# Holding back the later activation loads until the second third of a weight has landed

## The chip, the core and the metric

The kernel runs on one core of a Trainium2 chip. The metric is the device time of the whole kernel in microseconds (us). The engines are called PE (TensorE matmul), PEld (its weight loads), DVE (VectorE), ACT (ScalarE), POOL (GpSimd) and SP (SyncE, which here only issues transfers). PE's granted clock is the share of its full clock that it was given (1.00 is full). Before the change the median was 204.94 us over three runs, 204.71 to 204.94.

## The reference, cut to what matters

```python
xn = layernorm(x)                                  # x: 2048 tokens x 640
return x + linear_attention(xn, wqkv, wo) + gelu(xn @ w1 + b1) @ w2 + b2
```

The first 60 us of the kernel, the stage that the change touches, compute `gelu(xn @ w1 + b1)`, with `w1` of 640 x 1536. All numbers are bf16.

## The kernel before

The 2048 tokens are 16 tiles of 128. Tile t is loaded ("x*t*"), DVE computes its statistics and normalises it, the result is transposed (tiles 0 to 2 on PE, tiles 3 to 15 by a transposing DMA that SP issues), and PE multiplies it with W1. W1 comes in three thirds; the first is split over two queues. SP issues nearly all of it on its own queue, in this order:

```python
def dma_x(t, n):                       # x tiles t .. t+n-1, one DMA
    src = xv[t * P:(t + n) * P, :].rearrange("(t p) d -> p t d", p=P)
    Pl.ins("sync", lambda e: e.dma_start(x_in[:, t:t + n, :], src), writes=r_x[t:t + n], dma=True)
...
dma_x(0, 1)
dma_w("scalar", b1tmp[:], ...)                                   # ACT's queue
dma_w("scalar", W1[:, 0:KA, 0:FW], ..., r_W1A)                   # ACT's queue
dma_x(1, 1)
dma_w("sync", W1[:, KA:DT, 0:FW], ..., r_W1[0])                  # rest of the first third
dma_w1(1)                                                        # second third, 640 KB
dma_x(2, 1)
dma_w1(2)                                                        # last third, 640 KB
dma_x(3, 1)
dma_x(4, 2)                                                      # 320 KB
dma_x(6, 2)                                                      # 320 KB
dma_x(8, 4)                                                      # 640 KB
```

The rest of this stage in program order (DVE ran its part in this order in the trace of the kernel before: the statistics of tile 3 at 11.14 us, the first half of tile 4's at 12.64, the normalisation of tile 3 at 13.10):

```python
units(0, 2, JQ, 2 * JQ + 1)      # PE: tiles 0,1 with the second third (and one block of the last)
ln_stats(2)                      # DVE
ln_norm(2)
ln_stats(3)
xnT_copy(2, transp(2))           # PE transposes tile 2, DVE copies it
units(0, 2, 2 * JQ + 1, JT)
ln_next(3)                       # DVE: half statistics of tile 4, normalise tile 3, other half
xnT_dma(3)                       # SP: transposing DMA of tile 3
units(2, 1, 0, 10)               # PE: tile 2
units(3, 1, 0, 10)               # PE: tile 3, needs that DMA
units(2, 2, 10, JT)
for t in range(4, NT):           # DVE and SP: statistics, normalise, transposing DMA
    ...
units(4, 2, 0, 9)
...
```

Of the kernel before, what the change touches and what calls it, by code (L numbers as in the profile page):

```python
# [112 lines left out]
def bass_parallel_sum__linear_attn_block__dense_activation_gelu__prompt_kernel(  # L113
# [16 lines left out]
    Pl = Planner(nc)  # L130
# [7 lines left out]
    with contextlib.ExitStack() as es:  # L138
# [81 lines left out]
        r_W1 = [R_("W1_%d" % i) for i in range(NW1)]  # L220
# [30 lines left out]
        def dma_x(t, n):  # L251
            src = xv[t * P:(t + n) * P, :].rearrange("(t p) d -> p t d", p=P)
            Pl.ins("sync", lambda e: e.dma_start(x_in[:, t:t + n, :], src),
                   writes=r_x[t:t + n], dma=True)
# [7 lines left out]
        def dma_w1(i, eng="sync"):  # L262
            dma_w(eng, W1[:, :, i * FW:(i + 1) * FW], w1v[:, :, i * FW:(i + 1) * FW], r_W1[i])
# [7 lines left out]
        dma_x(2, 1)  # L271
        dma_w1(2)
        dma_x(3, 1)
        dma_x(4, 2)
        dma_x(6, 2)
        dma_x(8, 4)
# [555 lines left out]
```

## Time and profile before

| what | before |
|---|---|
| median time, three runs | 204.94 us |
| profiled span | 203.0 us |
| PE busy | 199.1 us, 98% |
| start of the first W1 product | 6.32 us |

The first fence is from the page of the kernel before: busy time of each engine, and the shares of the chain that ended last.

```profile
PE 199.1 (98%) x1317; PEld 121.8 (60%) x1329; DVE 123.0 (61%) x238; ACT 72.8 (36%) x139; POOL 14.4 (7%) x43
...
PE 96%; DVE 1%; DMA 1%; issue 0%; DVEq 0%
```

The second is the same chain in order of time (start us, length us, what).

```profile
0.80 2.27 DMA xPK<-in_A_x_dram
...
6.32 0.94 PE ps L407 x14
...
12.20 18.14 PE ps L375 x215
...
196.55 4.67 PE ps L726 x51
...
201.25 0.29 DVE out_l L729
```

The kernel waits for x0, normalises it, and from 6.32 us on the chain is PE's own work. So the time can change only if that run starts at another moment or gets a hole.

Next, the stretches of one microsecond (columns: stretch and its length; busy time of PE, PEld, DVE, ACT, POOL with instruction counts; granted PE clock; DMA share; GB/s), while the loads come in:

```profile
9.00:10.00 1.00, 1.00 (x13) 0.91 (x11) 0.90 (x3) 1.00 (x5) 0.22 (x1) 1.00 1.10 359
10.00:11.00 1.00, 1.00 (x12) 0.89 (x11) 0.24 (x2) 0.85 (x3) 0.57 (x1) 1.00 1.06 360
13.00:14.00 1.00, 1.00 (x14) 0.92 (x13) 0.94 (x3) 0.85 (x3) 0.40 (x1) 1.00 0.60 199
14.00:15.00 1.00, 1.00 (x22) 1.00 (x19) 0.95 (x3) 1.00 (x5) 0.66 (x2) 1.00 0.14 32
```

The transfers run at 360 GB/s until x8-11 drains at about 13.5 us. Last, SP's issue of x8-11 in the timeline (start, length), its time from issue to landing in the DMA view, and DVE's timeline around tile 4 (L331 statistics, L352 normalisation; the lines at 11.14, 12.64 and 13.10 are statistics of tile 3, first half of tile 4, and normalisation of tile 3):

```profile
5.93 0.98 SPq L253 DMA_DIRECT2D xPK<-in_A_x_dram  x1
```
```profile
xPK<-in_A_x_dram SPq DMA_DIRECT2D x1, 640.0 KB, 8.7
```
```profile
11.14 0.89 DVE L331 BATCH_NORM_STATS2 stats<-xPK 128x6 f32<-128x320 bf16 x2
12.64 0.48 DVE L331 BATCH_NORM_STATS2 stats<-xPK 128x6 f32<-128x320 bf16 x1
13.10 0.45 DVE L352 TENSOR_SCALAR xn_tm<-xPK,aggr,rstd 128x640 bf16<-128x640 bf16 x1
```

A line without brackets at its end had no wait worth noting before it: tile 4 was there when DVE came to it.

### The profile page before, as it was taken

The numbers are of one execution on the slowest core, as the hardware profiler recorded it, in microseconds if no ns is written. First come the engines' busy times: TensorE is split into PE (matmuls) and PEld (weight loads), VectorE is DVE, ScalarE is ACT, GpSimd is POOL, SyncE is SP. The second block draws the span as 40 slices with busy tenths as digits, with TensorE's granted clock in tenths as the row PEclk, the third lists the DMA queues.
The fourth block names the chain that finished last, engine by engine and source line by source line (L and its number), as shares of the span: only waits on it lengthen the run. The fifth ranks groups of instructions, "written<-read, shape, count | busy, mean of one in ns | idle before, by whom it ended". The sixth has DMA issues, their size and how long they took to land.

```text
span 203.0 us, 3442 instructions
## 1 busy us (share of the span) xinstructions
PE 199.1 (98%) x1317; PEld 121.8 (60%) x1329; DVE 123.0 (61%) x238; ACT 72.8 (36%) x139; POOL 14.4 (7%) x43
## 2 busy tenths in 40 slices
PE   7999999999999999999999999999999999999996
PEld 2799884444457777777756565444444444447775
DVE  4789682000006888999468899896793385356322
ACT  3589886666666544211143596100000000000000
POOL 3145443000000000000000000000000000000000
DMA  5975985999800000000289435115551966084402
GB/s 174 360 259 114 149 181 110 351 275 294 188 0 3 0 0 3 0 0 3 43 273 322 77 66 108 39 29 125 110 116 39 207 106 129 27 196 93 161 32 65
DMA packets 48134, 24.51 MB, mean 121 GB/s; under 512 B 33702, under 2 KB 48118, under 8 KB 48118
## 3 DMA queue, kind: packets, MB, share of 16 engines
q1 hardware_dynamic: 46094, 23.44, 46.4%
q10 hardware_dynamic: 2024, 0.86, 1.7%
q8 instruction: 10, 0.16, 0.3%
q14 instruction: 6, 0.05, 0.1%
HBM read 12.72 MB, written 2.62 MB: 76 GB/s over the span
## 4 chain that ended last, share of the span: by engine, by line
PE 96%; DVE 1%; DMA 1%; issue 0%; DVEq 0%
PE ps L748 27%; PE ps L375 25%; PE ps L524 11%; PE ps L557 11%; PE ps L569 11%; PE ps L690 7%; PE ps L726 2%; PE ps L407 1%; DMA xPK<-in_A_x_dram 1%; DVE stats L331 1%; PE ps L583 1%; PE ps L601 1%; PE ps L396 0%; DVE xn_tm L389 0%; DVE out_l L729 0%
## 5 line engine op out<-in xcount | busy, mean ns | idle before, releaser
L375 PE MATMUL ps<-xnT,W 128*128 128x256 bf16 (+2 forms) x372 | 50.2, 296 | 0.2
L375 PEld LDWEIGHTS ps<-xnT,W 128*128 128x128 bf16 x375 | 32.4, 98 | 17.3
L379 ACT ACTIVATE HG<-ps,b1c 128x256 bf16<-128x256 f32 (+2 forms) x75 | 37.3, 522 | 13.1 <-PE ps L375 11.3
L748 PE MATMUL ps<-HG,W 128*128 128x512 bf16 x177 | 39.2, 379 | 0.2
L748 PEld LDWEIGHTS ps<-HG,W 128*128 128x128 bf16 x180 | 17.6, 98 | 21.2
L569 PE MATMUL ps<-xnT,Wqkv 128*128 128x512 bf16 x96 | 22.2, 379 | 0.2
L524 PE MATMUL ps<-Wqkv,xnT 128*128 128x320 bf16 x160 | 21.9, 299 | 0.0
L557 PE MATMUL ps<-xPK,xn_tm 128*128 128x320 bf16 x160 | 21.9, 299 | 0.0
L524 PEld LDWEIGHTS ps<-Wqkv,xnT 128*128 128x128 bf16 x160 | 15.7, 98 | 6.2
L557 PEld LDWEIGHTS ps<-xPK,xn_tm 128*128 128x128 bf16 x160 | 15.7, 98 | 6.1
L754 DVE SCALAR_TENSOR_TENSOR W<-ps,b2c,xnT 128x512 bf16<-128x512 f32 x15 | 11.3, 751 | 8.9 <-PE ps L748 8.8
L748 PE MATMUL ps<-PQ,Msb 128*128 128x512 bf16 x73 | 16.4, 379 | 0.1
L569 PEld LDWEIGHTS ps<-xnT,Wqkv 128*128 128x128 bf16 x100 | 11.3, 118 | 8.5
L331 DVE BATCH_NORM_STATS2 stats<-xPK 128x6 f32<-128x320 bf16 x32 | 13.7, 468 | 4.4 <-DMA xPK<-in_A_x_dram 4.4
L508 ACT ACTIVATE xn_tm<-ps 128x512 bf16<-128x512 f32 x20 | 11.9, 597 | 9.4 <-PE ps L569 8.7
L511 DVE SCALAR_TENSOR_TENSOR PQ<-ps,xn_tm 128x512 bf16<-128x512 f32 x20 | 13.8, 692 | 2.1
L508 ACT ACTIVATE ek<-ps 128x640 bf16<-128x640 f32 x16 | 11.2, 703 | 9.2 <-PE ps L524 9.2
L511 DVE SCALAR_TENSOR_TENSOR xPK<-ps,ek 128x640 bf16<-128x640 f32 x16 | 13.2, 825 | 1.7
L516 DVE CAST b2c<-out_l 128x5 f32<-128x5 bf16 x1 | 0.2, 172 | 22.4 <-DMA out_l<-b2bc 22.4
L748 PEld LDWEIGHTS ps<-PQ,Msb 128*128 128x128 bf16 x75 | 7.3, 98 | 8.8
L618 DVE SCALAR_TENSOR_TENSOR xn_tm<-PQ,z_sb,xn_tm 128x512 f32<-128x512 bf16 x16 | 12.0, 750 | 0.4
L544 DVE TENSOR_TENSOR Msb<-Msb,xPK 128x640 f32<-128x640 f32 x14 | 11.6, 826 | 0.5
(64 smaller groups left out, 136.1 us busy)
## 6 DMA issues: line engine op xcount, KB each, us to landing
xPK<-in_A_x_dram SPq DMA_DIRECT2D x5, 640.0 KB, 6.9
Wqkv<-in_A_wqkv_dram SPq DMA_DIRECT2D x3, 800.0 KB, 7.0
W<-in_B_w_dram SPq DMA_DIRECT2D x1, 1920.0 KB, 14.8
out_dram<-xPK SPq DMA_DIRECT2D x3, 640.0 KB, 3.6
W<-in_B_w_dram SPq DMA_DIRECT2D x2, 640.0 KB, 6.7
xPK<-in_A_x_dram SPq DMA_DIRECT2D x4, 320.0 KB, 5.9
Wo<-in_A_wo_dram SPq DMA_DIRECT2D x1, 750.0 KB, 11.6
xPK<-in_A_x_dram SPq DMA_DIRECT2D x4, 160.0 KB, 4.4
```

What stands on the lines that cost most here:

```text
L331: Pl.ins(v, lambda e: e.bn_stats(stats[:, s, 6 * h:6 * h + 6], x_in[:, t, h * HW:(h + 1) * HW]), reads=[r_x[t]], writes=[r_stats[s][h]])
L375: Pl.ins("tensor", [(lambda e, k=k: e.matmul(bank(b, 0, w), W1[:, k, jb * P:(jb + 1) * P], xnT[:, k, tok], start=(k == 0), stop=(k == DT - ...
L379: Pl.ins("scalar", lambda e: e.activation(HG[:, jb, tok], bank(b, 0, w), ACT.Gelu_apprx_tanh, bias=b1c[:, jb:jb + 1]), reads=[B_[b], r_b1c ...
L508: Pl.ins("scalar", lambda e: e.activation(e2, src, ACT.Exp), reads=br, writes=[re])
L511: Pl.ins(v, lambda e: e.scalar_tensor_tensor(out=d2, in0=src, scalar=0.0, in1=e2, op0=ALU.max, op1=ALU.add), reads=br + [re], writes=[res_ ...
L524: fns.append(lambda e, k=k, h=h, b=b, t=t: e.matmul(bank(b + h, 0, HW), xnT[:, k, t * P:(t + 1) * P], Wqkv[:, k, D + h * HW:D + (h + 1) * ...
L544: Pl.ins(v, lambda e, t=t: e.tensor_tensor(out=zsum, in0=zsum, in1=PK[:, t, :], op=ALU.add), reads=[r_PK[t], r_zsum], writes=[r_zsum])
L557: Pl.ins("tensor", [(lambda e, t=t, h=h, b=b, f=f: e.matmul(bank(b + h, 0, HW), xn_tm[:, t, f * P:(f + 1) * P], PK[:, t, h * HW:(h + 1) * ...
L569: Pl.ins("tensor", [(lambda e, k=k, j=j, b=b: e.matmul(bank(b), Wqkv[:, k, j:D:DT], xnT[:, k, cc], start=(k == 0), stop=(k == DT - 1))) fo ...
L618: Pl.ins(v, lambda e: e.scalar_tensor_tensor(out=yv[c % 2], in0=pq, scalar=z_sb[:, j:j + 1], in1=yv[c % 2], op0=ALU.mult, op1=ALU.add), re ...
L690: return lambda e: e.matmul(bank(b + h, 0, HW), l, r[:, h * HW:(h + 1) * HW], start=(i == 0), stop=(i == JT + DT - 1))
L748: Pl.ins("tensor", lambda e, l=l, r=r, i=i: e.matmul(bank(b), l, r, start=(i == 0), stop=(i == JT + DT - 1)), reads=rd, writes=[B_[b]], ma ...
```

## The change

The idea is to keep 1280 KB of activations, which are needed later, from competing with W1 and x3, which are needed first. The diff is one line:

```diff
         dma_x(2, 1)
         dma_w1(2)
         dma_x(3, 1)
+        Pl.wait_event("sync", r_W1[1].w)
         dma_x(4, 2)
         dma_x(6, 2)
         dma_x(8, 4)
```

SP now stops after issuing x3 until W1's second third has landed, that is, until that load's semaphore has been raised 16 times. No byte and no instruction of another engine is added.

## The prediction

> **What bounds the kernel now.** TensorE. The page gives PE 199.1 of 203.0 us (98%). The chain of waits is 96% PE: from 6.32 us to the last eviction at 201.22 it is one unbroken run of matmuls, with only "issue" gaps of 0.05 us. The waits view lists a single PE wait, 1.3 us for the warm-up memset. Before that the chain is the load of x tile 0 (lands 3.07), statistics, normalisation, transposes. Only the start of that run, or a bubble in it, can move the time.
>
> **What the change does.** It adds one semaphore wait on SyncE, before the issue of x4-5, x6-7, x8-11 (1280 KB). The order view shows SP's instructions unchanged but for that wait. No byte is added or removed.
>
> Before, from the SP timeline and the DMA landing times (issue start + time to landing):
> - W1's second third: 2.2 + 6.1 = 8.3
> - x2: 2.73 + 6.1 = 8.8
> - W1's last third: 3.30 + 7.4 = 10.7
> - x3: 3.85 + 7.3 = 11.1
> - x4-5: 4.78 + 7.2 = 12.0; x6-7: 5.40 + 7.5 = 12.9; x8-11: about 6.0 + 8.7 = 14.7
>
> They land in the order of issue, spaced by their size at 360 GB/s (the windows view, flat from 6 to 13 us). [...] So x4 to x11 stand *behind* everything that the change wants to favour; they take no bandwidth from it. I expect no earlier landing of W1 or x3 (under 0.2 us), and PE waits for none anyway. (W1's last third is first needed near 11.2 us.)
>
> **After.** SP stalls from about 4.75 to 8.4, then issues the three loads with the same durations (0.58, 0.6, about 0.9): done near 10.6. An unloaded load takes 2.3 us to land in this trace (x0), of which about 1.2 us pass before data moves. So x4's packets are queued by about 9.6 us, while x3 and W1's last third still move. No hole opens in the DMA stream, or one of a few tenths. Landings: x4-5 12.0 to 12.3, x6-7 12.9 to 13.2, x8-11 14.6 to 15.0.
>
> **Slack.** DVE starts statistics of tile 4 at 12.64, of tile 6 at about 15.5, of tile 8 at 18.1: slack 0.6, 2.6, 3.5 us. SP's next work, the transposing load of tile 3, is issued at 13.57, after SP is free again (10.6). It lands at 16.3 and is needed by PE near 17.1. Nothing reaches PE.
>
> **Predicted:** 204.9 us, range 204.4 to 205.5. Faster by over 2%: 0.5%; within 2%: 99%; slower: 0.5%.
>
> **Right or wrong in the profile after:** start of the first W1 matmul still 6.3 us; W1 thirds and x3 land within 0.2 us of before; SP's three load issues begin near 8.4; DMA rate still about 360 GB/s to 13 us, with no slot below 250; statistics of tile 4 start within 0.3 us of 12.64; PE's waits view stays a single entry; everything from 20 us on is shifted by under 0.3 us.
>
> **What would make it wrong.** If a re-issued load takes far longer to get its first packet moving than 2.3 us, x4 lands after 13.3, DVE falls behind, the transposes of tiles 4 and 5 slip past PE's need near 20 us, and up to 1 us is lost. If queued loads do disturb those ahead of them, the first stage ends some tenths earlier.

That argument is the order of the landings in the trace (8.3, 8.8, 10.7, 11.1, 12.0, 12.9, 14.7 us) and their spacing at 360 GB/s; that the loads behind take no bandwidth was the inference from it. The forecast's 1.2 us before data moves is an estimate too; for x0 the trace has 1.04 us (0.80 to 1.84).

## The result, and the profile after

The changed kernel took 204.82 us (median of six runs, 204.64 to 205.88) against 204.92 us (six runs, 204.71 to 205.18). Ratios here are the mean time of one kernel's fast runs over the mean of the other's fast runs of the same rounds, so not quite the ratio of those medians: it is 1.0005, with a 95% interval of 0.9983 to 1.0027. Two more sets of timed rounds, on other occasions, gave 0.9996 (0.9974 to 1.0018) and 1.0011 (0.9989 to 1.0034). The change makes no difference that these runs can resolve.

The page's lines after the change, which answer to the first fence:

```profile
PE 200.2 (98%) x1329; PEld 121.9 (60%) x1329; DVE 123.0 (60%) x238; ACT 72.9 (36%) x139; POOL 14.4 (7%) x43
...
PE 96%; DVE 1%; DMA 1%; issue 0%; DVEq 0%
```

PE's larger busy sum is the 12 matmul records that are missing before (1317 of 1329), not more work. SP's waits show the new wait (us in total, times, longest):

```profile
SPq L253 <- DMA W<-in_B_w_dram: 3.7, 1, 3.7
```

SP's issue of x8-11 in the timeline, and its landing in the DMA view:

```profile
9.77 0.47 SPq L253 DMA_DIRECT2D xPK<-in_A_x_dram  x1
```
```profile
xPK<-in_A_x_dram SPq DMA_DIRECT2D x1, 640.0 KB, 5.6
```

So it is issued 3.8 us later (5.93 to 9.77), and lands 0.7 us later (5.93 + 8.7 = 14.6; 9.77 + 5.6 = 15.4). The queue's backlog has swallowed most of the delay. The same stretches as before:

```profile
9.00:10.00 1.00, 1.00 (x15) 0.92 (x13) 0.68 (x2) 1.00 (x5) 0.10 (x1) 1.00 0.91 289
10.00:11.00 1.00, 1.00 (x12) 0.90 (x10) 0.41 (x2) 0.91 (x3) 0.52 (x2) 1.00 0.92 272
13.00:14.00 1.00, 1.00 (x13) 0.91 (x11) 0.99 (x4) 0.92 (x2) 0.81 (x2) 1.00 0.94 324
14.00:15.00 1.00, 1.00 (x22) 1.00 (x20) 0.90 (x4) 0.94 (x4) 0.24 (x2) 1.00 0.23 86
```

The transfer rate dips between 9 and 11 us (289 and 272 GB/s against 359 and 360), and the missing bytes come after 13 us. DVE around tile 4:

```profile
11.64 0.88 DVE L332 BATCH_NORM_STATS2 stats<-xPK 128x6 f32<-128x320 bf16 x2
13.10 0.48 DVE L332 BATCH_NORM_STATS2 stats<-xPK 128x6 f32<-128x320 bf16 x1
13.59 0.45 DVE L353 TENSOR_SCALAR xn_tm<-xPK,aggr,rstd 128x640 bf16<-128x640 bf16 x1
```

Here everything is 0.5 us later than before, and still without a wait for tile 4. Something ahead of tile 4 was late. That something is x2: DVE waits for it in front of tile 2's statistics, in the kernel before and in the one after:

```profile
8.81 0.89 DVE L331 BATCH_NORM_STATS2 stats<-xPK 128x6 f32<-128x320 bf16 x2 [0.52 <-DMA xPK<-in_A_x_dram]
```
```profile
9.32 0.89 DVE L332 BATCH_NORM_STATS2 stats<-xPK 128x6 f32<-128x320 bf16 x2 [0.84 <-DMA xPK<-in_A_x_dram]
```

Whether the change did it was the first question for the experiments.

### The profile page after: what moved, and what is told of

Same layout as the page of the kernel before. It is cut to its first block, busy times and chain, and to the rows that moved or that the text cites. A ratio compares the mean times of both kernels' runs of the same rounds, so it can differ in the third digit from the quotient of the medians.

```text
span 203.4 us, 3454 instructions
## 1 busy us (share of the span) xinstructions
PE 200.2 (98%) x1329; PEld 121.9 (60%) x1329; DVE 123.0 (60%) x238; ACT 72.9 (36%) x139; POOL 14.4 (7%) x43
## 4 chain that ended last, share of the span: by engine, by line
PE 96%; DVE 1%; DMA 1%; issue 0%; DVEq 0%
PE ps L749 27%; PE ps L376 25%; PE ps L558 11%; PE ps L525 11%; PE ps L570 11%; PE ps L691 7%; PE ps L727 2%; PE ps L408 1%; DMA xPK<-in_A_x_dram 1%; DVE stats L332 1%; PE ps L584 1%; PE ps L602 1%; PE ps L397 0%; DVE xn_tm L390 0%; PE ps L319 0%
## 5 line engine op out<-in xcount | busy, mean ns | idle before, releaser
L570 PE MATMUL ps<-xnT,Wqkv 128*128 128x512 bf16 x100 | 22.8, 379 | 0.0
L749 PE MATMUL ps<-PQ,Msb 128*128 128x512 bf16 x75 | 16.7, 379 | 0.0
L512 DVE SCALAR_TENSOR_TENSOR xPK<-ps,ek 128x640 bf16<-128x640 f32 x16 | 13.2, 825 | 1.7
```

The lines of the kernel that those rows point to most:

```text
L512: Pl.ins(v, lambda e: e.scalar_tensor_tensor(out=d2, in0=src, scalar=0.0, in1=e2, op0=ALU.max, op1=ALU.add), reads=br + [re], writes=[res_ ...
L570: Pl.ins("tensor", [(lambda e, k=k, j=j, b=b: e.matmul(bank(b), Wqkv[:, k, j:D:DT], xnT[:, k, cc], start=(k == 0), stop=(k == DT - 1))) fo ...
L749: Pl.ins("tensor", lambda e, l=l, r=r, i=i: e.matmul(bank(b), l, r, start=(i == 0), stop=(i == JT + DT - 1)), reads=rd, writes=[B_[b]], ma ...
```

## The experiments

Each kernel was made from the kernel before or after by the diff shown (the repeats have none); all gave correct results. The largest help for reading them was a table that is not a view of the profile but worked out from the traces' records: the semaphore of each load in the table is raised 16 times, read as once by each of the core's 16 DMA engines, and the table gives the moments of the first and of the last of the 16. For W1's second third, 640 KB, the last comes 1.2 to 2.0 us after the first in the kernel before (7.17 / 8.33 to 7.10 / 9.13). "PE's gap" is the distance between the weight loads on both sides of tile 3's first product less the usual 0.056 us.

```
first / last engine, us    W1 second third   x2           x3            x4-5          x8-11         PE's gap before tile 3
before                     7.17 / 8.33       7.62 / 8.79   9.95 / 11.12  10.85 / 12.02  13.58 / 14.64  0.00
before, trace 2            7.15 / 8.68       7.63 / 9.14   9.94 / 11.43  10.86 / 12.37  13.55 / 14.88  0.13
before, trace 3            7.05 / 8.84       7.52 / 9.31   9.96 / 11.65  10.86 / 12.55  13.55 / 15.07  0.06
before, trace 4            7.10 / 9.13       7.57 / 9.60   9.95 / 11.93  10.85 / 12.84  13.54 / 15.31  0.35
after                      7.11 / 8.83       7.60 / 9.29   9.88 / 11.44  11.38 / 12.33  13.99 / 15.37  0.17
after, trace 2             7.22 / 9.16       7.66 / 9.64   9.93 / 11.76  11.62 / 12.63  14.37 / 16.24  0.32
after, trace 3             7.08 / 8.94       7.56 / 9.40   9.84 / 11.57  11.36 / 12.42  14.02 / 16.88  1.22
after, trace 4             7.37 / 9.13       7.81 / 9.59  10.09 / 11.73  11.65 / 12.62  14.33 / 16.40  0.43
```

The weight-load records allow one more reading, since there are 1329 of them in every trace. Held against the first trace before, load by load, each of the other twelve traces falls behind by an amount that grows until about 27 us and then stays the same to 0.01 us up to the end: 0.17, 0.36 and 0.64 us in the other traces before, 0.38, 0.65, 1.31 and 0.72 us in the four after. So nothing later than this stage adds time or gives it back.

### Repeats of both kernels

No edit; three more traces of each kernel.

> The kernel before, unchanged, for a second trace. Open: in the first pair of traces W1's second third landed at 8.3 us before and at 8.8 after, x2 at 8.8 and 9.3, x3 at 11.15 and 11.5, and the statistics of tile 3 began at 11.14 and 11.64. Theory A (a wait placed behind these loads in the same queue cannot slow them; this is scatter from run to run): the landing of W1's second third moves by some tenths between repeats of one kernel, so that 8.3 to 8.8 is covered by either. Theory B (the wait itself shifts them by 0.3 to 0.5 us): this repeat stays at 8.2 to 8.4 and the repeat of the changed kernel at 8.7 to 8.9. Both: 204.5 to 205.3 us, tile 7's transpose lands about 24.4 and PE's weight loads show no thin spot between 25 and 26 us.

> The changed kernel, unchanged, for a second trace and five timed rounds. Theory A: ratio 1.000 within 0.002; landing of W1's second third anywhere from 8.2 to 8.9. Theory B: it lands at 8.7 to 8.9 again. Either way SP's load issues begin 0.1 us after it, the DMA rate from 9 to 11 us dips to 270 to 300 GB/s (before: 360), because engines that finished their share of W1 early have nothing queued, and the statistics of tile 4 start at 12.6 to 13.2.

> The kernel before, unchanged, for a third trace. So far x2 landed at 8.83 and 9.14 us before, at 9.25, 9.65 and (wait on x3) 9.34 with a wait, W1's second third at 8.30, 8.71 against 8.81, 9.12, 8.91. Theory A (scatter): x2 lands anywhere in 8.8 to 9.6. Theory B (the wait makes them 0.3 to 0.4 us later): it stays at or under 9.15. Both: tile 3's transpose lands 7.45 us after x2, and PE waits for it before tile 3 only if x2 is later than about 9.1.

> The changed kernel, unchanged, for a third trace. Theory A: x2 lands anywhere in 8.8 to 9.6. Theory B: at or over 9.25. Both: x4-5 land 0.85 to 0.95 us after x3, as in the kernel before, so that the statistics of tile 4 don't wait for them; tile 3's transpose lands 7.45 us after x2.

> The kernel before, a fourth trace. So far x8-11 landed at 14.63, 14.85, 15.10 us (last of the 16 engines) and tile 3's transpose took 2.7 us each time. Expected again: x8-11 at 14.5 to 15.2, transpose 2.7 us, PE's gap before tile 3 at most 0.3 us, x2 at 8.8 to 9.5.

> The changed kernel, a fourth trace and five more timed rounds. So far x8-11 landed at 15.37, 16.21, 16.88 us, and in the third trace tile 3's transpose, issued at 14.16, took 3.6 us behind that tail and PE waited 1.2 us for it. Expected if that late tail comes from the wait: x8-11 at 15.3 or later again (before: 15.1 or earlier); PE's gap before tile 3 between 0 and 1.3 us; ratio of the timed runs 0.998 to 1.003.

Times: before 204.59, 204.78, 205.06 us (one run each); after 204.98 us (median of six, ratio 0.9996), 205.72 us (one run), 205.19 us (median of six, ratio 1.0011).

Small misses first: in the second trace before, tile 7's transpose landed at 25.3 us, not 24.4 (that scatters too); in the second trace after, W1's second third landed at 9.16, over the range of either theory (8.9 at most), and the statistics of tile 4 began at 13.44, over the 13.2 that was expected; and in the fourth trace before, x2, x8-11 and PE's gap were each just over their expected range (9.60, 15.31, 0.35).

**The landing of W1 and x2 scatters.** Theory B falls as it was stated (8.2 to 8.4 us without the wait, x2 at or under 9.15): the kernel before alone puts W1's second third anywhere from 8.33 to 9.13 us and x2 from 8.79 to 9.60 us. That covers three of the four traces after; the second is 0.03 and 0.04 us over. The mean of the four is 0.27 us later with the wait for either load, while the ranges overlap, so a small shift is neither shown nor excluded. The first engine's share is steady (7.05 to 7.37); the slowest engine makes the difference. Nothing lands earlier with the wait, so no trace shows the gain that the change aimed at.

**x4-5 is not delayed.** It lands 0.90 to 0.94 us after x3 before and 0.85 to 0.89 us after x3 with the wait. Only its first engine is later (10.85 to 10.86 us before, 11.36 to 11.65 after; 0.90 to 0.92 us after x3's first before, 1.50 to 1.69 after): from that difference, the quick engines have nothing queued for an estimated 0.6 to 0.8 us. That is the dip in the rate. The slowest engine, which decides the landing, is still busy with W1 and x3 when the new load is issued (in the first trace after at 8.85, while the last engines for W1's last third and x3 came at 11.03 and 11.44), so it loses nothing. Between 10 and 11 us the dip reached 182 GB/s in the second trace after and 230 in the fourth, below the 250 that the prediction allowed and the 270 to 300 expected for the second.

**x8-11 is later in every trace:** 14.64, 14.88, 15.07, 15.31 us before, 15.37, 16.24, 16.88, 16.40 us after. That it is later fits the dip, and a second one between 12 and 13 us (253 to 343 GB/s in the four traces after, 362 to 366 before). Why its slowest engine then trails by up to 2.9 us (14.02 to 16.88) was not settled. The packet records show a candidate: a fetch of instructions, one packet of 16 KB on a queue of its own that takes 0.96 to 1.13 us, starts near x8-11's end in all eight traces (13.06 to 13.76 us before, 13.85 to 15.14 after). In the DMA view of the third trace after, from 15 to 16 us, it is this line:

```profile
q8 instruction: 1, 0.02, 6.0%
```

There the fetch ran from 15.14 to 16.10, and x8-11's last engine reported 1.44 us after the load's last data packet (15.44), against 0.34 to 0.50 us in the other seven traces. Whether the fetch sat on that engine the records don't tell, so this is not shown.

**Where the slack ends.** Tile 3's transposing DMA lands 7.42 to 7.54 us after x2 in seven of the eight traces. So x2, not x4, leads the tight chain (x2, statistics and normalisation of tile 2, tile 3, transpose), with x3 just behind (it had landed 0.02 to 0.05 us before DVE came to it in the traces before), and PE has a gap of up to 0.35 us there *before* the change when x2 is late. The eighth trace is the third one after: there the transpose lands 8.32 us after x2. In that kernel's trace, the waits of the weight loads and their timeline (in brackets the idle time before, and what ended it) are:

```profile
PEld ps L376 <- DMA xnT<-xn_tm: 1.2, 1, 1.2
```
```profile
14.92 1.66 PEld L376 LDWEIGHTS ps<-xnT,W 128*128 128x128 bf16 x29
17.76 2.29 PEld L376 LDWEIGHTS ps<-xnT,W 128*128 128x128 bf16 x41 [1.18 <-DMA xnT<-xn_tm]
```

The transpose was issued at 14.16 and took 3.6 us instead of 2.7, behind x8-11, whose last engine finished at 16.88: 22 of the transpose's packets, begun from 15.93 us on, all ended between 16.85 and 16.90, the longest after 0.94 us, where the earlier ones took under 0.06. PE lost 1.2 us, and that execution is the slowest of the eight that were traced (205.72 us). So in that execution a late x8-11 cost time. x8-11 is later in all four traces with the wait, which makes the cost more likely; that the wait made this long tail isn't shown. The timed runs, which scatter from 204.5 to 206.3 us for the unchanged kernel, can't resolve a mean cost.

### The wait set later: on x3 instead of W1's second third

```diff
-        Pl.wait_event("sync", r_W1[1].w)
+        Pl.wait_event("sync", r_x[3].w)
```

> The same three loads wait for x3 to have landed (about 11.2 us) in place of W1's second third. This queue then holds nothing but what the change wants to favour until 11.2 us. Theory 1 (one queue works in order; the later loads never took bandwidth from the earlier ones): W1's thirds, x2 and x3 land as before within the scatter (W1's last third 10.5 to 11.0), the DMA rate falls under 100 GB/s for about 1 us after 11.2, x4-5 land near 14.1 against 12.0, the DVE chain is 1.3 to 1.6 us late, and since the transposes of tiles 5 and 7 had only about 0.6 to 0.8 us to spare, PE loses 0.5 to 1.0 us: ratio 1.0025 to 1.005. Rival (the queued loads do take bandwidth, and the change's gain is only hidden): W1's last third and x3 land 0.5 us or more earlier than before. Rival 2 (large slack as the prediction's table has it for the late tiles, 2.6 us and more): ratio 1.000, PE's weight loads without a thin spot.

Measured: 207.01 us (median of four), ratio 1.0113 (1.0072 to 1.0154). W1's last third landed at 11.07 and x3 at 11.46, inside the scatter of the kernel before (10.66 to 11.47 and 11.12 to 11.93), although nothing at all was queued behind them. Their first engines, which scatter less, finished at 9.55 and 9.97, against 9.49 to 9.51 and 9.94 to 9.96 before. This is the cleanest test of the change's intent: the rival that queued loads take bandwidth from those ahead falls. The stretches show the hole (50, then nothing, then 55 GB/s):

```profile
10.00:11.00 1.00, 1.00 (x11) 0.90 (x10) 0.44 (x2) 0.93 (x3) 0.52 (x2) 1.00 0.14 50
11.00:12.00 1.00, 1.00 (x11) 0.90 (x10) 0.69 (x2) 0.86 (x3) 0.20 (x1) 1.00 0.00 0
12.00:13.00 1.00, 1.00 (x14) 0.92 (x13) 0.90 (x4) 0.62 (x2) 0.28 (x2) 1.00 0.42 55
```

The loss of 2.3 us (0.0113 x 205) is over twice what was expected. One of the four timed runs (208.93 us) had a mean granted clock of 0.992; the other three, at full clock, are 1.8 us over the kernel before. That is still too much, for two reasons. First, x4-5, issued at 11.48 into an empty queue, landed at 15.65, 4.2 us later; the expectation had 2.9. Second, the path to PE was not through tiles 5 and 7. DVE's timeline and the waits of the weight loads:

```profile
11.67 0.88 DVE L332 BATCH_NORM_STATS2 stats<-xPK 128x6 f32<-128x320 bf16 x2
15.67 0.49 DVE L332 BATCH_NORM_STATS2 stats<-xPK 128x6 f32<-128x320 bf16 x1 [2.46 <-DMA xPK<-in_A_x_dram]
16.08 0.43 DVE L353 TENSOR_SCALAR xn_tm<-xPK,aggr,rstd 128x640 bf16<-128x640 bf16 x1
```
```profile
PEld ps L376 <- DMA xnT<-xn_tm: 2.5, 1, 2.5
```

The first half of tile 4's statistics waits for x4, and tile 3's normalisation (16.08) stands behind it in DVE's order. So a late x4 makes *tile 3* late, and PE comes to tile 3 at 16.7 us.

### The same, with tile 3 normalised first

```diff
-        ln_next(3)
+        ln_norm(3)
         xnT_dma(3)
+        ln_stats(4)
```

> The kernel with the wait for x3, with VectorE's order changed: tile 3 is normalised (and its transpose issued) before tile 4's statistics, not behind their first half. In the trace of the wait for x3, tile 4's first statistics waited 2.46 us for x4 and tile 3's normalisation stood behind them, so PE waited 2.6 us for tile 3. Theory P (VectorE's program order alone carries the delay to PE): the normalisation of tile 3 starts near 13.1, its transpose lands near 17, PE's wait before tile 3 falls under 0.5 us; the wait moves to tiles 4 and 5 and is about 1 us, ratio to before 1.005 to 1.008. Theory Q (the queue's order holds it up as well): the transpose is issued at about 14.3, when SP has issued x8-11, but its packets stand behind those 1280 KB; it lands at 18.2 to 18.9, PE still waits 1.5 to 2.2 us, ratio 1.009 to 1.011.

Measured: 209.64 us (median of four), ratio 1.0197 (1.0148 to 1.0246). Tile 3 was now normalised at 13.95, before x4 had landed, and SP issued its transpose at 14.42; but it took 6.1 us and landed at 20.52, behind x8-11 (last engine 19.84). Theory P falls, theory Q holds in kind and was too mild: PE's gap was 3.6 us. In the DMA view and the timeline of this kernel:

```profile
14.42 1.30 SPq L449 DMA_TRANSPOSE xnT<-xn_tm  x1
```
```profile
xnT<-xn_tm SPq DMA_TRANSPOSE x1, 6.1
```

So VectorE's order was only one of two locks on tile 3, and SP's queue the other; opening one alone did not help. The time rose by more than the gap, because the granted clock fell to half afterwards (three of the four timed runs had a mean clock of 0.992; the fourth, at full clock, took 207.39 us, about what the kernel with VectorE's old order took):

```profile
22.00:23.00 1.00, 1.00 (x12) 1.00 (x11) 0.96 (x4) 0.67 (x3) 0.70 (x2) 0.50 0.81 162
23.00:24.00 1.00, 1.00 (x12) 1.00 (x10) 0.61 (x3) 0.67 (x3) 0.06 (x1) 0.50 0.71 143
```

Forty weight loads of this stretch took 3.8 us (20.75 to 24.55) against 2.23 in the kernel before (16.64 to 18.87). Gap and slow pace are 3.6 + 1.6 = 5.2 us; the profiled execution was 210.14 us, 5.1 us over the kernel before's median of 205.07. In this trace a gap of 3.6 us was followed by 3.4 us at half pace (21.25 to 24.65). The length of the gap alone doesn't tell when this happens: in the experiment with x4 to x7 on another queue, below, a gap of 2.0 us was followed by 3.4 us at half clock, while in the profiled execution of the kernel that waits for x3 a gap of 2.6 us was not (1.00 in every stretch from 16 to 22 us). What decides it was not tested.

### x2 ahead of W1's second third

```diff
-        dma_w1(1)
         dma_x(2, 1)
+        dma_w1(1)
```

(made in the kernel before, without the wait)

> The kernel before with the load of x2 issued ahead of W1's second third. Theory: the tight chain of this stage starts with x2's landing, not with x4's. x2 lands at 6.9 to 7.6 (8.8 to 9.2 before), W1's second third 0.45 us later than before (8.8 to 9.2, needed near 9.0: PE may wait up to 0.2 us there), tile 2 is normalised 1.5 us earlier, tile 3 is then bound by x3's landing and gains 0.1 to 0.3 us only. PE's wait before tile 3 is gone. Time: ratio 0.998 to 1.001. If x4's landing is the binding one instead, tile 3's normalisation does not move (13.1 to 13.5) and its statistics of tile 4 are preceded by a wait for x4.

Measured: 205.25 us (median of six), ratio 1.0007 (0.9981 to 1.0033). x2 landed at 7.17 us, W1's second third at 9.25, with a PE gap of 0.26 us in front of its first use (both just over what was expected). DVE's timeline shows tile 2's statistics at 8.27, and those of tile 3 now waiting for x3:

```profile
8.27 0.87 DVE L331 BATCH_NORM_STATS2 stats<-xPK 128x6 f32<-128x320 bf16 x2
...
11.61 0.89 DVE L331 BATCH_NORM_STATS2 stats<-xPK 128x6 f32<-128x320 bf16 x2 [0.95 <-DMA xPK<-in_A_x_dram]
```

As expected, the tight chain lets go of x2, but x3 takes its place at once, PE's gap before tile 3 is 0.07 us (0.00 to 0.35 before), and 0.26 us is lost at W1. This confirms that x4 doesn't bind, and this exchange wins nothing: both places are needed about when they come. Other orders were not tried.

### x4 to x7 on another queue

The loads of x4-5 and x6-7 are issued by ACT, behind its first activation in program order; x8-11 stays. (In the kernel before, without the wait.)

```diff
-        dma_x(4, 2)
-        dma_x(6, 2)
...
         Pl.ins("scalar", ... ACT.Gelu_apprx_tanh ..., writes=[r_b1c])
+        dma_x(4, 2, "scalar")
+        dma_x(6, 2, "scalar")
```

> The kernel before with the loads of x4-5 and x6-7 issued from the scalar engine's queue instead of the sync engine's, at nearly the same time (3.4 to 4.8 us), x8-11 left where it is. Theory 1 (within one queue later loads wait their turn; in another queue they share): these 640 KB now compete with W1 and x3: W1's second third lands 1 to 2 us later (9.3 to 10.3 against 8.3), W1's last third and x3 likewise, x4-5 land far earlier than 12.0 (about 7.5), PE stalls near 9 us, and the kernel loses 0.7 to 2 us: ratio 1.003 to 1.010. Rival (queued loads share bandwidth whatever their queue): landings move by less than 0.4 us and the time stays.

Measured: 207.82 us (median of four), ratio 1.0125 (1.0091 to 1.0159), 2.6 us lost, more than the expected 1.003 to 1.010. One thing was not as planned: ACT's sequencer issued the loads at 2.00 and 2.44 us, ahead of the activation that precedes them in the program (ACT was loading that activation's table from 1.93 to 3.21), not at 3.4 to 4.8. So the comparison at equal issue time is lost, but one load still decides: the rest of W1's first third was issued at 1.73, before them. On the single queue it landed at 6.3 to 7.0 us in all four traces before; here it landed at 8.70. A later load on another queue delayed an earlier one, which no load on the same queue was seen to do. PE waited for it:

```profile
PE ps L405 <- DMA W<-in_B_w_dram: 1.7, 1, 1.7
```

W1's second third landed at 11.26 instead of 8.3 to 9.1. Packets of two queues do go out side by side in the traces: in the kernel before, where W1's first part is on ACT's queue, 19 packets of SP's queue and 13 of ACT's started between 4.0 and 4.1 us. In the profiled execution PE did not wait for W1's second third, though: the gap of 2.0 us at the first third and a slow pace after it make up the whole loss. PE's clock halved for 3.4 us (8.81 to 12.23), and three of the four timed runs show it (mean clock 0.992; the fourth, at full clock, took 206.82 us):

```profile
10.00:11.00 1.00, 1.00 (x12) 1.00 (x11) 0.33 (x2) 0.69 (x2) 0.00 (x0) 0.50 1.09 356
```

### The same queue, with the wait

```diff
         h_first(1, [0, 1, 2, 3], r_xnTA1)
+        Pl.wait_event("scalar", r_W1[1].w)
+        dma_x(4, 2, "scalar")
+        dma_x(6, 2, "scalar")
```

(in place of the two lines behind the activation)

> x4-5 and x6-7 on the scalar engine's queue as in the experiment before, but issued only when W1's second third has landed (and behind the first eight gelus), so near 9.3 us. There the same idea of waiting should pay, because loads on another queue do share: the 2.6 us that moving them cost come back. Theory 1: W1's first third lands at 6.2 to 7.1 (8.7 without the wait), its second third at 8.3 to 9.1 (11.3), PE's gap before the second half of the first W1 products falls from 2.0 us to under 0.3; x4-5 land at 12.3 to 13.3, which costs at most some tenths before tile 3: ratio to before 0.999 to 1.004. Rival (what cost 2.6 us is the issue from the scalar engine or the lower clock, not the sharing): ratio stays over 1.008.

Measured: 206.03 us (median of four), ratio 1.0046 (1.0017 to 1.0076). The rival (over 1.008) falls: with loads on a second queue, holding them back wins 0.8% over not doing so (1.0125 to 1.0046). (The loads also stand behind the first eight gelus now, so it is the later issue that is tested, not the semaphore alone.) But the ratio stayed above the expected 0.999 to 1.004, because the loads went out at 10.05 only and were then under way beside x8-11, which had passed them on SP's queue (landed at 13.97): x4-5 landed at 14.76, DVE waited 1.02 us for it, and PE had a gap of 1.1 us before tile 3. In this trace the first third of W1 landed at 7.54, later than in any trace of the kernel before, which cost PE 0.8 us (under 0.3 was expected), and the second third at 9.38, over the expected 9.1; neither x load on ACT's queue had been issued by then, and why is open.

## Why the prediction was right, and where its steps were not

- **PE bounds the kernel, and only the start of its run or a hole in it counts.** Right. Each loss in the experiments was seen as a gap of PE, or as its slow clock after a gap, and none came after 27 us. But "PE waits for none" of W1's thirds doesn't hold in every execution: in the fourth trace before, where the second and the last third landed at 9.13 and 11.47, PE lost 0.06 and 0.16 us at their first uses.
- **"x4 to x11 stand behind everything that the change wants to favour; they take no bandwidth from it."** Right, and the reason for the missing gain. With nothing queued behind W1's last third and x3 until 11.5 us, they landed no earlier. With x4 to x7 on a second queue, W1's second third was over 2 us later.
- **"W1 thirds and x3 land within 0.2 us of before."** Wrong as a check: the kernel before itself scatters by 0.8 us. One trace of each kernel would have suggested that the wait *delays* W1 by 0.5 us; in four of each the ranges overlap, and no delay is shown.
- **"No hole opens in the DMA stream, or one of a few tenths"; no slot below 250.** Half right. There is a dip (272 GB/s in the first trace, 182 in the second), since the quick engines run dry, but the slowest engine doesn't, so x4-5 follows x3 at the same distance as before.
- **"Landings: x4-5 12.0 to 12.3", "x8-11 14.6 to 15.0".** Missed: x4-5 landed at 12.33 to 12.63, x8-11 at 15.4 to 16.9.
- **Statistics of tile 4 "within 0.3 us of 12.64", everything from 20 us on "shifted by under 0.3 us".** Missed in all four traces after (13.10 to 13.44; 0.32 to 1.31 us), and poor checks: the kernel before itself scatters from 12.64 to 13.42 and by 0 to 0.64 us.
- **"An unloaded load takes 2.3 us to land."** That was x0, 160 KB, whose first packet started 1.04 us after its issue (0.80 to 1.84), not 1.2. x4-5, 320 KB with more loads behind it, took 4.2 us from its issue into an empty queue.
- **"Slack 0.6, 2.6, 3.5 us" and "needed by PE near 17.1. Nothing reaches PE."** Too kind. PE comes to tile 3 at 16.4 to 16.8 us, and the transpose lands at 16.2 to 17.1 in the kernel before: the spare time is 0.2 us or none. The table of slack looked at when DVE uses a tile, but not at what stands behind that use in DVE's order and in SP's queue. The predicted time survived because the delay of x4 was nearly zero, not because there was room for it; that part is luck.
- **"PE's waits view stays a single entry."** True in the first two traces after, not in the other two (1.0 and 0.2 us before tile 3), and of little use: that view takes PE's modelled ends, which hid the gap of 0.32 us in the second. The waits of the weight loads showed it.

That the mean cost is zero isn't shown. The gaps before tile 3 would give about 0.4 us (mean 0.54 us after, 0.14 before, of which one trace makes most); the upper ends of the three intervals are 0.4 to 0.7 us (1.0018 to 1.0034), so a cost of some tenths is neither shown nor excluded.

## What to carry to other kernels

Within one queue the loads landed in the order of issue here, and holding back a later load on that queue did not speed up an earlier one (x3 landed at 11.46 us with nothing behind it, 11.12 to 11.93 before); it only let the quick DMA engines run dry (289 and 272 GB/s against 359 and 360). Holding back paid where the loads sat on different queues, because there a later load had delayed an earlier one (W1's first third at 8.70 us, against 6.3 to 7.0): it won back 1.6 us of 2.6. Before moving a load, ask not only who uses it, but what stands behind that user in its engine's order and what stands behind the load in its queue; and take several traces of the unchanged kernel before reading a shift of half a microsecond as an effect.
